# State-space block and SiLU layer on one core: decay factors of the first two units spread over the partitions by products with 0/1 matrices, and a new instruction list

## The chip, the core and the metric

The kernel runs on one core of one Trainium2 chip. A core has a matrix engine (TensorE, PE in the profile; its weight loads are PEld), a vector engine (VectorE, DVE), an activation engine (ScalarE, ACT), a general engine (GpSimd, POOL), and a queue engine (SyncE, SP) that here only issues DMA transfers. They run side by side and wait for one another by semaphores. On-chip data lies in a memory of 128 partitions; TensorE writes its results to a separate accumulator memory (PSUM). The metric is the device time of one execution in microseconds (us), smaller is better. A product of float32 operands shows in the trace as two matmul records on PE; one of operands marked float32r shows as one.

## What is computed

The reference is a chunked state-space scan per batch and head, whose output goes through a two-layer network with a SiLU between.

```python
batch, H, S, D, N = 4, 8, 768, 32, 16      # x: (4,8,768,32)  a: (4,8,768)  B, C: (4,8,768,16)
log_a = log(clip(a, 1e-6, 1)); state = 0
for each chunk of the sequence:
    cum = cumsum(log_a[chunk])
    L   = exp(cum_i - cum_j), causal                  # product of a between j and i
    y   = ((C B^T) * L) @ x  +  (C @ state) * exp(cum)
    state = exp(sum log_a) * state + sum_j exp(cum_last - cum_j) * B_j x_j
x2  = y as (3072, 256)
h   = x2 @ w_in                                       # w_in: (256, 2048)
out = (h * sigmoid(h)) @ w_out                        # w_out: (2048, 256)
```

The two weight matrices arrive as 64-bit floats and have to be rebuilt as 32-bit ones on the chip. The output is (3072, 256) in float32.

## The kernel before, in words

The work is cut into 12 units of 256 sequence positions (3 per batch). For a unit, the state-space part is: load B and C in two layouts (`Ln`, `Lt`), x (`Lx`) and the factors a in two layouts; run prefix products of a along the sequence, once as a table of 128 x 512 per half unit (`E`, f_E, line 481, a scan on DVE against a `diag` pattern) and once per chunk (`P01`/`P`, lines 446 and 453); multiply B by the last column of the table (`B`, line 489, on POOL); transpose C and B (`T` line 494 on DVE, `tp` line 500 on PE); form the small products of B, C and x (`g0` line 556, `D`/`gd` line 542), multiply with the table (`M`, line 571), carry the state (`S`, lines 584 and 586, and `SM`, line 594), and add up the unit's output (`Y`, lines 607 and 616), which ScalarE copies out (`X0` line 646, `y` line 652).

The network then takes the outputs two units at a time. The first pair (units 0 and 1) goes through it in plain float32: `s,u,j` (f_s1, line 676) is the first layer for unit u and the 256 hidden columns of weight block j, `si` (line 682) the SiLU, `n` (line 744) the second layer. The other five pairs go through products of operands split into three float32r parts: `a` and `d` (line 785) with `ax` (796) and `dg` (806) for the first layer; `h` (812), `l` (633), `e` (636) split its result; `f` (766) is the second layer.

Each of the 16 weight blocks (`lw,n`: 0 to 7 of w_in, 8 to 15 of w_out, 512 KB each, in 7 buffers) is rebuilt by two ScalarE steps (`u` line 283, `v` line 286), three DVE steps (`w,n,0` line 292, `w,n,1` line 296, `w,n,2` line 299) and an addition on GpSimd (`W`, line 310, some in two halves), then split for the later pairs (`H` line 314, `Wd` line 322 on ScalarE, `Wl` line 319 on GpSimd, `We` line 326 an accumulating DMA that GpSimd issues).

**Where the factors a come from.** Units 2 to 11 read them from two scratch tensors in DRAM, `az` and `ac`: all of a is loaded by four DMAs (`ir`, line 350), clamped on GpSimd (`AA`, line 429), and written out (`AD`, lines 435 and 437). Units 0 and 1 cannot wait for that. For the per-chunk products, `ip,u,q` (line 346) loads 8 heads' factors with each row repeated onto 16 partitions, 128 KB, straight into 128 partitions; DVE clamps it (`P01,u,0`, line 442) and scans it (`P01,u,1`, line 446). For the table, `ia` (line 342) loads a as 32 rows of 2 x 64; DVE clamps it (`A`, line 415), PE transposes it (`AT`, line 420), DVE copies the result (`AU`, line 424); `as,u,k` (f_AS) then spreads each column to 128 x 512, once on DVE (line 464) and three times on ScalarE (line 466), and `ab,u,k` (f_Ab, line 471) transposes that by four PE transposes, so that every partition holds the wanted row.

**What sets the order.** There is no scheduler: the string SCHEDULE lists some 1,400 tokens, each a call of one of these functions, and each engine runs its own instructions in the list's order. A token `z` is dummy matmuls that keep PE running (lines 408 and 410). The third or last number of `Ln`, `Lt`, `Lx`, `ip`, `lw` names the queue that issues the DMA: 0 SyncE, 1 ScalarE, 2 GpSimd. SLOTS lists, for each kind of buffer, which of its places each new tile takes. The list's first tokens are

```text
c1 ip,0,0 Ln,0,0,0,1 ci ia lw,0 z,1 cp cI z,1 ch z,1 z,0,6 Lt,0,1,2,1 z,0,6 z,0,6 z,1 Lt,0,1,0,1 Lt,0,1,3,1 z,1
Lt,0,1,1,1 cd lw,2 co z,1 Ln,0,0,1,1 z,1 Ln,1,0,0,0 P01,0,0 ct A ip,1,0 z,1 P01,0,1 Lx,0,0,0 Lx,0,1,0 AT u,0 AU
Ln,1,0,1,0 ca z,1 as,0,0 z,1 as,1,1 z,1 ab,0,0 Ln,1,1,0,0 z,0,6 cP as,0,1 w,0,0 T,0,1 Ln,1,1,1,0 C,0 as,1,0 Lx,1,0,0
```

The small constants are built at the start: `ci` (idle, line 355), `c1`/`cd` (diag, 366 to 372), `cI` (identity, 361), `ch` and `cP` (head mask and par, 381 to 389), `cp` and `co` (patterns for the scans, 376 to 393), `ct` (line 358, a one-column SiLU that makes ScalarE load its function table).

Of the kernel before, what the change touches and what calls it, by code (L numbers as in the profile page):

```python
# [13 lines left out]
ALU = mybir.AluOpType  # L14
# [16 lines left out]
ce,2,1 tq,2 W,9,1,0 n,2 w,11,2 si,0,3 u,6 Lt,3,0,3,0 ce,2,0 E,2,1 Wl,4 lw,7 W,10,1,0 n,1 E,2,0 lw,12 AD,1 n,1 v,7 n,1
w,5,1 P,2 C,2 g0,2 B,2 W,5,1,0 gd,2 b,2,0 La,3,0,0 M,2,1 b,2,1 Lt,3,0,1,0 Lx,3,0,0 La,3,1,0 AD,2 u,7 u,12 Ln,3,0,1,0
W,11,1,0 S,2,0 w,6,0 Lt,3,0,2,0 w,7,2 Lt,3,0,0,0 Lt,4,1,0,0 M,2,0 Ln,3,0,0,0 n,1 Lt,4,1,1,0 Lp,3,0 ce,3,0 S,2,1 S,2,2
H,11 lw,14 w,7,0 w,7,1 n,2 s,0,5 ce,3,1 w,6,2 SM,2,1 E,3,0 SM,2,0 Y,2 Lx,3,1,0 si,0,5 n,1 v,12 n,1 W,7,1,0 n,1 H,1 H,9
E,3,1 lw,13 y,2,0 n,1 y,2,1 s,0,7 B,3 xh,2 x,2,0 T,3,0 H,5 g0,3 Wd,0 w,6,1 P,3 H,10 Lt,4,0,3,0 w,12,2 gd,3 La,4,0,0
si,0,7 b,3,0 M,3,1 w,12,0 Wd,9 Lt,4,0,1,0 Lt,4,0,2,0 b,3,1 La,4,1,0 S,3,0 S,3,1 W,6,1,0 Lt,4,1,2,0 s,0,6 Wl,11 si,0,6
v,13 C,3 M,3,0 S,3,2 w,12,1 Wl,5 Lt,4,1,3,0 SM,3,0 SM,3,1 x,2,1 u,13 H,8 Lp,4,0 n,1 We,0 s,1,6 W,12,1,0 Y,3 T,4,1
lw,15 w,13,2 n,2 Wl,3 y,3,0 Ln,4,0,0,0 Lt,4,0,0,0 y,3,1 xh,3 n,1 w,13,0 Lx,5,1,0 x,3,0 x,3,1 S,3,3 a,1,0 E,4,1
Ln,4,0,1,0 si,1,6 s,1,5 w,13,1 We,2 v,15 Lx,4,0,0 P,4 AD,3 n,1 u,15 ce,4,1 W,13,1,0 T,4,0 w,15,0 ax,1,0 u,14 E,4,0
d,1,0 ce,4,0 si,1,5 H,6 v,14 w,14,0 H,7 dg,1,0 Lx,4,1,0 Wl,10 H,12 w,14,1 C,4 w,15,1 Lp,5,0 s,1,7 w,14,2 B,4 si,1,7  # L40
g0,4 W,14,1,0 h,1,0 gd,4 M,4,1 n,1 Lx,5,0,0 b,4,0 b,4,1 S,4,0 n,1 Wd,1 S,4,1 S,4,2 Wd,12 Lt,5,0,2,0 Wl,1 We,1 n,2
M,4,0 Lt,5,1,3,0 Wd,5 SM,4,0 La,5,1,0 n,1 SM,4,1 Y,4 Wl,8 w,15,2 e,1,0 n,1 Wd,3 Wl,7 y,4,1 H,13 f,1 a,1,1 y,4,0 We,4
# [843 lines left out]
```

## Time and profile before

| quantity | value |
|---|---|
| median of 3 runs | 331.68 us (331.28 to 333.41) |
| the profiled execution's own time | 331.95 us |
| its span on the core, from first to last recorded event | 330.2 us |
| mean granted TensorE clock | 0.998 |
| instructions recorded | 7573 |
| PE, PEld busy | 319.5, 243.8 us |
| DVE, ACT, POOL busy | 240.8, 207.4, 88.8 us |
| DMA | 95,817 packets, 30.83 MB, 80,088 packets under 512 bytes |

The page gives each engine's busy time and its course in 40 slices of 8.25 us. The chain of waits names the work that ended last at each moment; the timeline lists instructions in order of time; the windows give busy time by stretch. A busy PE need not be a PE at its peak, since the ends of matmul records are modelled.

### The profile page before, as it was taken

Reading aid. Unit: us, or ns where it says so; the run is one execution under the profiler, and the core shown is the slowest. Engines: PE = TensorE matmul, PEld = TensorE weight load, DVE = VectorE, ACT = ScalarE, POOL = GpSimd, SP = SyncE. Lnnn points to the kernel's source line nnn. Section 1 sums busy time; section 2 is a strip of 40 time slices with the busy share of each in tenths; the row PEclk is TensorE's granted clock in tenths of the full one; section 3 lists DMA queues with packets and bytes.
Section 4 is the critical chain, followed back from the end, with each engine's and each line's share of the span. In section 5 each row is a group of like instructions: output and inputs, shape, how many; then the busy total and the mean of one; then the engine's idle time right before and its main releaser. Section 6 shows DMA issues by size and latency. Waiting matters only on the chain.

```text
span 330.2 us, 7573 instructions
## 1 busy us (share of the span) xinstructions
PE 319.5 (97%) x3086; PEld 243.8 (74%) x3086; DVE 240.8 (73%) x314; ACT 207.4 (63%) x323; POOL 88.8 (27%) x96
## 2 busy tenths in 40 slices
PE   7699999999999999999999999999999999999995
PEld 3478746665667778877878878778887788888883
DVE  4979899999957972978589469688648534555563
ACT  3689928578787558565756566655664737474441
POOL 2367853978969510020010100200000000000000
PEclk9999999999999999999999999999999999999999
DMA  6799699594696991412422441450003100005002
GB/s 170 121 339 222 184 219 206 142 193 102 129 185 98 196 173 35 99 47 45 99 25 64 74 97 24 92 102 11 2 0 65 18 0 2 0 0 89 0 0 64
DMA packets 95817, 30.83 MB, mean 93 GB/s; under 512 B 80088, under 2 KB 87000, under 8 KB 95784
## 3 DMA queue, kind: packets, MB, share of 16 engines
q1 hardware_dynamic: 90632, 25.58, 36.1%
q0 software_dynamic: 2480, 4.39, 7.4%
q10 hardware_dynamic: 2672, 0.39, 0.7%
q8 instruction: 24, 0.39, 0.5%
q14 instruction: 9, 0.07, 0.1%
HBM read 22.81 MB, written 3.34 MB: 79 GB/s over the span
## 4 chain that ended last, share of the span: by engine, by line
PE 88%; DVE 4%; DMA 3%; SPq 2%; ACT 1%; issue 1%; POOL 1%; DVEq 0%
PE hp L766 28%; PE ga L785 17%; PE gb L785 17%; PE hp L676 7%; PE o_ps L766 6%; PE hp L744 5%; PE ga L616 2%; PE ga L556 2%; PE ga L607 1%; DMA raw<-in_moe_w_in_dram 1%; DVE s2k L292 1%; DMA s2k<-in_C_dram 1%; PE ga L542 1%; PE gb L607 1%; SPq L258 1%
## 5 line engine op out<-in xcount | busy, mean ns | idle before, releaser
L766 PE MATMUL hp<-r4k,s2k 128*128 128x512 f32 x400 | 113.3, 394 | 0.0
L766 PEld LDWEIGHTS hp<-r4k,s2k 128*128 128x128 f32 x400 | 74.4, 188 | 16.5 <-issue 0.6
L633 DVE SCALAR_TENSOR_TENSOR r4k<-r4k,r4k 128x1024 fp32r<-128x1024 f32 x40 | 50.9, 1278 | 30.1 <-PE hp L766 16.8
L636 DVE SCALAR_TENSOR_TENSOR r4k<-r4k,r4k 128x1024 fp32r<-128x1024 f32 x40 | 49.7, 1247 | 27.2 <-ACT r4k L812 15.2
L785 PE MATMUL ga<-raw,s2k 128*128 128x512 f32 x240 | 62.8, 397 | 0.0
L785 PE MATMUL gb<-raw,s2k 128*128 128x512 f32 x240 | 61.8, 393 | 0.0
L785 PEld LDWEIGHTS ga<-raw,s2k 128*128 128x128 f32 x240 | 44.6, 188 | 12.2 <-issue 1.2
L785 PEld LDWEIGHTS gb<-raw,s2k 128*128 128x128 f32 x240 | 44.4, 188 | 11.2 <-ACT gb L796 1.0
L812 ACT ACTIVATE r4k<-r4k 128x1024 fp32r<-128x1024 f32 x40 | 41.8, 1055 | 4.3 <-PE hp L766 2.6
L796 ACT ACTIVATE ga<-ga 128x1024 f32<-128x1024 f32 x20 | 20.2, 1009 | 32.6 <-PE ga L785 32.6
L796 ACT ACTIVATE gb<-gb 128x1024 f32<-128x1024 f32 x20 | 20.2, 1008 | 17.9 <-PE gb L785 16.9
L766 PE MATMUL o_ps<-r4k,s2k 128*128 128x512 f32 x80 | 31.2, 396 | 0.0
L744 PE MATMUL hp<-r4k,s2k 128*128 128x512 f32 x64 | 29.8, 600 | 0.7 <-POOL s2k L310 0.7
L676 PE MATMUL hp<-r4k,s2k 128*128 128x256 f32 x128 | 29.5, 382 | 0.0
L489 POOL TENSOR_TENSOR BT<-bn,ab 128x256 f32<-128x256 f32 x10 | 9.4, 939 | 72.0 <-PE hp L766 27.8
L676 PEld LDWEIGHTS hp<-r4k,s2k 128*128 128x128 f32 x128 | 23.9, 190 | 5.0 <-issue 1.0
L310 POOL TENSOR_TENSOR s2k<-s2k,s2k 128x512 uint32<-128x512 uint32 (+1 forms) x19 | 24.1, 1277 | 11.3 <-DVE s2k L299 5.8
L520 POOL TENSOR_TENSOR cw<-ct,pfx 128x256 f32<-128x256 f32 x9 | 9.5, 1053 | 64.8 <-DVE pfx L453 64.8
L806 ACT ACTIVATE r4k<-ga 128x1024 f32<-128x1024 f32 x20 | 20.5, 1024 | 9.8 <-PE ga L785 4.3
L481 DVE TENSOR_TENSOR_SCAN ab<-ab,diag 128x512 f32<-128x512 f32 x20 | 26.0, 1316 | 0.8 <-DMA ab<-az 0.8
L806 ACT ACTIVATE r4k<-gb 128x1024 f32<-128x1024 f32 x20 | 20.4, 1022 | 6.8 <-PE gb L785 5.7
L319 POOL TENSOR_TENSOR s2k<-s2k,s2k 128x512 fp32r<-128x512 f32 x16 | 24.0, 1568 | 0.8 <-ACT s2k L314 0.8
(118 smaller groups left out, 399.0 us busy)
## 6 DMA issues: line engine op xcount, KB each, us to landing
ab<-az SPq DMA_DIRECT2D x20, 256.0 KB
raw<-in_moe_w_in_dram SPq DMA_DIRECT2D x8, 512.0 KB
raw<-in_moe_w_out_dram SPq DMA_DIRECT2D x8, 512.0 KB
s2k<-s2k POOLq DMA_DIRECT2D x16, 256.0 KB, 5.4
out_dram<-r4k SPq DMA_DIRECT2D x44, 64.0 KB
xt<-in_x_dram SPq DMA_DIRECT2D x20, 128.0 KB
pz<-ac SPq DMA_DIRECT2D x10, 130.0 KB
bn<-in_B_dram SPq DMA_DIRECT2D x20, 64.0 KB
```

Source lines behind the costliest of these rows:

```text
L310: nc.gpsimd.tensor_tensor(out=dst[:, :, fs].bitcast(U32), in0=u[:, :, fs], in1=v[:, :, fs], op=ALU.add)
L319: nc.gpsimd.tensor_tensor(out=t, in0=f32(WK[n, "h"]), in1=WT[n], op=ALU.add)
L481: nc.vector.tensor_tensor_scan(out=o, data0=src, data1=diag.rearrange("p h t -> p (h t)"), initial=0.0, op0=ALU.mult, op1=ALU.add)
L633: nc.vector.scalar_tensor_tensor(out=l, in0=f32(h), scalar=BACK, in1=y, op0=ALU.mult, op1=ALU.add)
L636: nc.vector.scalar_tensor_tensor(out=d, in0=f32(h), scalar=-(BACK + 1.0), in1=y, op0=ALU.mult, op1=ALU.subtract)
L676: nc.tensor.matmul(out=hp[:, i], lhsT=WT[j][:, kc, 128 * i:128 * i + 128], rhs=XM[:, 2 * kc:2 * kc + 2, u], start=(kc == 0), stop=(kc == K ...
L744: nc.tensor.matmul(out=NP["o"][m], lhsT=WT[8 + f // 2][:, f % 2, 128 * m:128 * m + 128], rhs=GT[0, f // 2][:, f % 2], start=(f == 0), stop ...
L766: nc.tensor.matmul(out=ACC[P, 2 * (p == "d") + m], lhsT=WK[8 + f // 2, p][:, f % 2, 128 * m:128 * m + 128], rhs=rhs, start=(f == 0 and p ! ...
L785: nc.tensor.matmul(out=o, lhsT=WK[j, q][:, kc, 128 * i:128 * i + 128], rhs=xs[:, 2 * kc:2 * kc + 2], start=(start and q == "h" and kc == 0 ...
L796: nc.scalar.activation(t, t, AF.Copy, scale=1.0 + Z)
L806: nc.scalar.activation(g, t, AF.Silu, scale=BACK)
L812: nc.scalar.activation(t, GT[G, i], AF.Copy, scale=-LESS * Z)
```

## The change

Units 0 and 1 get their factors in another way, and the whole list (SCHEDULE and SLOTS) is a new one.

- `ip` is now one DMA: 8 heads x 512 positions, 16 KB, on 8 partitions. GpSimd clamps each unit's half (`PA`), one product on PE with the 0/1 matrix `spread` (8 x 128) puts each head's row on 16 partitions (`pb`), and DVE scans it from PSUM (`P01`). The two 128 KB loads and DVE's two clamps are gone.
- `ia` loads the 32 chunk rows of all 8 heads, 64 KB, into partitions 96 to 127 of a 128 x 512 tile `ar`; `zr` sets the other 96 partitions to zero; DVE clamps the tile (`A`). `ab,u,k` is one product on PE of the full height of 128 with 128 columns of the 0/1 matrix `pick`, instead of a spread copy and four transposes. `AT`, `AU` and the four `as` copies are gone.
- GpSimd builds `pick` (128 x 512, token `cs`) and `spread` (8 x 128, `c2`) by a memset and two selects each.
- In the new list one of the four `ir` loads is the third DMA that SyncE issues; `lw,2` comes ahead of `lw,0`; `ct` comes after `ab,1,0`, so that the first ScalarE function is a `ce` copy; and the order of the rest differs throughout. The number of `z`, `s`, `n`, `a`, `d`, `f` steps' matmuls is the same.

```diff
-    ach = small([32, 2, Q])
-    aT = small([128, 8, 4])
+    ar, pr = small([128, H, Q]), small([H, 2 * UT])
+    pick, spread = small([128, 4 * 128]), small([H, 128])
...
     def i_a():
-        nc.sync.dma_start(out=ach, in_=bass.AP(tensor=a.tensor, offset=a.offset,
-                                               ap=[[Q, 8], [2 * S, 4], [S, 2], [1, Q]]))
-    def i_p(u, q):
-        QUEUES[q].dma_start(out=pa[u], in_=bass.AP(tensor=a.tensor, offset=a.offset + UT * u,
-                                                   ap=[[S, H], [0, N], [1, UT]]))
+        nc.sync.dma_start(out=ar[96:128], in_=bass.AP(tensor=a.tensor, offset=a.offset,
+                                                      ap=[[Q, 32], [S, H], [1, Q]]))
+    def c_rest():
+        nc.vector.memset(ar[0:96], 0.0)
+    def i_p(q):
+        QUEUES[q].dma_start(out=pr, in_=bass.AP(tensor=a.tensor, offset=a.offset, ap=[[S, H], [1, 2 * UT]]))
...
+    def band(t, n, w, p0=0):
+        nc.gpsimd.memset(t, 1.0)
+        nc.gpsimd.affine_select(out=t, in_=t, pattern=[[1, n]], compare_op=ALU.is_ge,
+                                fill=0.0, base=w * p0, channel_multiplier=-w)
+        nc.gpsimd.affine_select(out=t, in_=t, pattern=[[-1, n]], compare_op=ALU.is_ge,
+                                fill=0.0, base=w - 1 - w * p0, channel_multiplier=w)
...
     def f_A():
-        nc.vector.tensor_scalar(out=ach, in0=ach, scalar1=1.0, scalar2=1e-6, op0=ALU.min, op1=ALU.max)
-        nc.vector.memset(ach[:, :, 0:1], 0.0)
-    def f_AT():
...
-    def f_AU():
...
+        nc.vector.tensor_scalar(out=ar, in0=ar, scalar1=1.0, scalar2=1e-6, op0=ALU.min, op1=ALU.max)
+        nc.vector.memset(ar[:, :, 0:1], 0.0)
...
-    def f_P01(u, what):
-        if what == 0:
-            nc.vector.tensor_scalar(out=pz01[u][:, :, 1:], in0=pa[u].rearrange("p (c t) -> p c t", c=4),
-                                    scalar1=1.0, scalar2=1e-6, op0=ALU.min, op1=ALU.max)
-            return
+    def f_PA(u):
+        nc.gpsimd.tensor_scalar(out=pz01[u][:, :, 1:], in0=pr[:, UT * u:UT * u + UT].rearrange("p (c t) -> p c t", c=4),
+                                scalar1=1.0, scalar2=1e-6, op0=ALU.min, op1=ALU.max)
+    def f_pb(u):
+        AB["p", u] = t = take("hp", [128, 4, Q + 1])
+        nc.tensor.matmul(out=t.rearrange("p c t -> p (c t)"), lhsT=spread, rhs=pz01[u].rearrange("p c t -> p (c t)"),
+                         start=True, stop=True)
+    def f_P01(u):
...
-                                     data0=pz01[u].rearrange("p c t -> p (c t)"),
+                                     data0=AB["p", u].rearrange("p c t -> p (c t)"),
...
-    def f_AS(u, k):
...
     def f_Ab(u, k):
         AB[u, k] = t = take("hp", [128, H, Q])
-        for j in range(4):
-            nc.tensor.transpose(out=t[:, 2 * j:2 * j + 2].rearrange("p h t -> p (h t)"),
-                                in_=AS[u, k][:, j].rearrange("p c q -> p (c q)"), identity=ident)
+        f = 128 * (2 * u + k)
+        nc.tensor.matmul(out=t.rearrange("p h t -> p (h t)"), lhsT=pick[:, f:f + 128],
+                         rhs=ar.rearrange("p h t -> p (h t)"), start=True, stop=True)
```

The new list begins

```text
ip,0 ia cs ci ir,3 c1 ch c2 Ln,0,0,0,1 z,1 cI z,1 z,1 Lt,0,1,2,1 Lt,0,1,0,1 zr z,0,6 z,0,6 A z,0,6 z,1 cd lw,2 cP cp
Lt,0,1,1,1 z,1 z,1 PA,0 z,1 z,1 z,1 pb,0 Lt,0,1,3,1 ab,0,0 T,0,1 ab,0,1 P01,0 Ln,0,0,1,1 ab,1,1 Lx,0,0,0 lw,0 Lx,0,1,0
PA,1 ce,0,0 v,2 C,0 u,2 z,1 u,0 z,1 z,0,6 Ln,1,0,1,0 E,0,0 Ln,1,1,0,0 E,0,1 E,1,1 Ln,1,0,0,0 ce,0,1 w,0,0 B,0,0 z,0,6
B,0,1 z,0,6 Ln,1,1,1,0 tp,0 tq,0 D,0 g0,0 S,0,0 Lt,3,1,1,0 S,0,1 v,0 pb,1 w,2,0 S,0,2 Lx,1,0,0 M,0,1 M,0,0 Lx,1,1,0
ir,0 ab,1,0 ct co lw,1 w,2,1 w,2,2 SM,0,1 SM,0,0 B,1,1 tp,1 ce,1,1 tq,1 Y,0 ce,1,0 X0,0,0 S,0,3 X0,0,1 E,1,0 P01,1
lw,3 W,2,2,0 W,2,2,1 H,2 u,1 w,0,2 B,1,0 w,0,1 g0,1 v,1 lw,4 D,1 S,1,0 S,1,1 S,1,2 v,3 SM,1,0 M,1,0 s,0,2 M,1,1 w,1,0
SM,1,1 W,0,2,0 ir,1 w,1,2 lw,10 u,3 Lt,3,1,3,0 W,0,2,1 ir,2 w,1,1 s,0,0 si,0,0 C,1 u,4 S,1,3 w,3,0 W,1,2,0 lw,9 lw,8
v,4 w,3,2 W,1,2,1 w,3,1 Y,1 lw,11 X0,1,1 X0,1,0 u,10 s,0,1 w,4,0 Ln,2,1,1,0 H,0 s,1,2 Wl,2 w,4,2 AA,0 Ln,2,0,1,0
si,0,2 si,0,1 s,1,0 u,9 v,10 w,4,1 AD,4 w,9,0 Ln,2,0,0,0 W,3,1,0 w,10,0 v,9 W,4,1,0 si,1,2 H,3 s,1,1 si,1,1 u,8 s,1,4
```

More of the change, by code (lines that the diff above doesn't have):

```diff
@@ L94 @@
-os,5,1,0,0 or,5,1,1 os,5,1,1,1
+ip,0 ia cs ci ir,3 c1 ch c2 Ln,0,0,0,1 z,1 cI z,1 z,1 Lt,0,1,2,1 Lt,0,1,0,1 zr z,0,6 z,0,6 A z,0,6 z,1 cd lw,2 cP cp
+Lt,0,1,1,1 z,1 z,1 PA,0 z,1 z,1 z,1 pb,0 Lt,0,1,3,1 ab,0,0 T,0,1 ab,0,1 P01,0 Ln,0,0,1,1 ab,1,1 Lx,0,0,0 lw,0 Lx,0,1,0
+PA,1 ce,0,0 v,2 C,0 u,2 z,1 u,0 z,1 z,0,6 Ln,1,0,1,0 E,0,0 Ln,1,1,0,0 E,0,1 E,1,1 Ln,1,0,0,0 ce,0,1 w,0,0 B,0,0 z,0,6
+B,0,1 z,0,6 Ln,1,1,1,0 tp,0 tq,0 D,0 g0,0 S,0,0 Lt,3,1,1,0 S,0,1 v,0 pb,1 w,2,0 S,0,2 Lx,1,0,0 M,0,1 M,0,0 Lx,1,1,0
@@ L330 @@
     QUEUES = (nc.sync, nc.scalar, nc.gpsimd)
-    ach = small([32, 2, Q])
-    aT = small([128, 8, 4])
+    ar, pr = small([128, H, Q]), small([H, 2 * UT])
+    pick, spread = small([128, 4 * 128]), small([H, 128])
     araw, azt = small([NCH, H, Q]), small([NCH, H, Q])
     acp = large([NCH, H, Q + 1])
-    pa = [small([128, UT]) for _ in range(2)]
-    pz01, pfx01 = ([small([128, 4, Q + 1]) for _ in range(2)] for _ in range(2))
+    pz01 = [small([H, 4, Q + 1]) for _ in range(2)]
+    pfx01 = [small([128, 4, Q + 1]) for _ in range(2)]
     one01 = small([128, 4, Q + 1])
```

177 lines of the change are left out of this document (82 added, 95 removed), and 6 rows, old and new, of the table SLOTS.

## The prediction, made before the changed kernel was run

> **What bounds the kernel now.** I read the page first, for the engines' shares and their course over the 40 slices, then the chain of waits in order of time.
>
> ```profile
> PE 319.5 (97%) x3086; PEld 243.8 (74%) x3086; DVE 240.8 (73%) x314; ACT 207.4 (63%) x323; POOL 88.8 (27%) x96
> POOL 2367853978969510020010100200000000000000
> ```
>
> ```profile
> 2.47 4.75 DMA raw<-in_moe_w_in_dram
> 7.24 2.79 SPq L258
> 10.07 0.97 SPq L243
> 11.08 4.26 DMA s2k<-in_C_dram
> 19.01 3.65 PE hp L676 x16
> 24.07 10.56 PE hp L676 x48
> ...
> 72.61 0.86 PE hp L744 x2
> ...
> 320.10 4.53 PE hp L766 x20
> ```
>
> The columns of the chain are start, length, and what the end hung on. Up to 15.3 us it is loads: a weight block, then x, B and C on SyncE's queue. From 19.0, where the first `s` begins, it is PE almost without a break to 324.6. So the time is a front of 19 us in which little of PE's work gets done, some 305 us of PE's own work, and a tail of 5.6 us. The change leaves PE's real work as it is; it can gain by starting the `s` steps earlier and by removing gaps after that. The windows say how large the gaps are (columns: stretch, its length, busy us and instructions of each engine, clock, DMA share, GB/s).
>
> ```profile
> 10.00:15.00 5.00, 2.75 (x72) 1.70 (x72) 5.00 (x11) 2.28 (x7) 1.44 (x3) 1.00 0.81 104
> 15.00:20.00 5.00, 4.14 (x159) 3.30 (x160) 4.16 (x10) 2.95 (x9) 3.66 (x5) 1.00 0.87 252
> 45.00:50.00 5.00, 4.77 (x67) 2.61 (x67) 4.87 (x8) 2.63 (x7) 4.10 (x4) 1.00 1.09 209
> 50.00:60.00 10.00, 9.58 (x184) 6.11 (x183) 9.93 (x15) 7.46 (x18) 4.65 (x4) 1.00 0.80 189
> 60.00:70.00 10.00, 9.28 (x116) 6.11 (x116) 9.89 (x15) 6.78 (x15) 8.90 (x8) 1.00 0.84 171
> ```
>
> Between 45 and 70 us PE is idle 0.23 + 0.42 + 0.72 = 1.37 us, while DVE is busy nearly all the time. The clock is granted in full. That, and whatever stalls hide under the modelled ends of the matmuls, is what a better sequence has to win behind the front.
>
> **The front, part by part.** The timeline, with start, length and what ended the idle time before:
>
> ```profile
> 1.93 0.35 POOL L362 TENSOR_SCALAR_AFFINE_SELECT ident<-ident 128x128 f32<-128x128 f32 x1 [0.29 <-DVE ident L361]
> 4.04 1.28 ACT L358 ACT_TABLE_LOAD   x1 [4.04 <-DMA s2k<-in_B_dram]
> 4.19 0.29 DVE L442 TENSOR_SCALAR s2k<-s2k 128x256 f32<-128x256 f32 x1 [2.06 <-DMA s2k<-in_a_dram]
> 4.94 0.21 DVE L415 TENSOR_SCALAR s2k<-s2k 32x128 f32<-32x128 f32 x1 [0.46 <-DMA s2k<-in_a_dram]
> 5.20 0.69 DVE L446 TENSOR_TENSOR_SCAN s2k<-s2k,s2k 128x260 f32<-128x260 f32 x1
> 6.01 0.43 DVE L464 COPY s2k<-s2k 128x512 f32<-128x512 f32 x1
> 6.67 0.60 PE L471 MATMUL hp<-ident,s2k 128*128 128x128 f32 x4
> 7.82 1.65 ACT L466 ACTIVATE s2k<-s2k 128x512 f32<-128x512 f32 x3
> 7.95 0.43 DVE L292 TENSOR_SCALAR s2k<-s2k 128x512 f32<-128x512 f32 x1 [1.38 <-ACT s2k L283]
> 8.29 0.64 DVE L494 STREAM_TRANSPOSE ct<-s2k 128x256 f32<-128x256 f32 x1
> 9.11 3.43 DVE L481 TENSOR_TENSOR_SCAN ab<-hp,diag 128x512 f32<-128x512 f32 x3
> 15.39 0.51 PE L500 MATMUL o_ps<-ident,s2k 128*128 128x128 f32 x2 [1.69 <-DMA s2k<-in_C_dram]
> 15.61 1.22 DVE L481 TENSOR_TENSOR_SCAN ab<-hp,diag 128x512 f32<-128x512 f32 x1
> ```
>
> *PE.* The trace has no 512-column plain float32 product in the front; the `n` steps have (72.61 us, two records, 0.86 us). So each `ab` costs 0.86 us against 0.60 for four transposes: four cost 1.0 us more. The two `pb`, 260 columns, cost by width 0.44 each, and `AT` goes. All this replaces PE time that holds dummies or stands idle (2.25 us from 10 to 15 and 0.86 from 15 to 20 in the windows). I cost it at nothing; without that cover it would be 1.9 us.
>
> *GpSimd* gains `pick`: a memset and two selects of 128x512. The 128x128 select took 0.35; four times that, 1.4, is a ceiling for each, 0.35 the floor; with a fixed part in it I take 0.7, so 2.1 in all. With `spread` (three steps of at most 0.35) that is 3.1 us at the start of GpSimd's queue, where `c1` and `ch` stood, and `PA,0` runs at 5 to 6 us, with `pb` behind it. That is in time for the first scans, next.
>
> *DVE* loses two clamps (2 x 0.29), the small clamp, `AU` and the 0.43 copy, and gains the clamp of 128x512 (0.43, as L292 has it) and a memset of 96x512 while it waits for the load. Its order is now: `A` after the load at about 4.9, `cd` and small constants (0.8), `T` (0.64), `P01` (0.69), then the three `E` scans. That lets them start at 7.5 to 8.5 against 9.11. But L292 and L296 of one weight block, done before them until now, come behind them: some 0.7 given back. `E,1,0`, at 15.61 before, comes at 15.2 or so. *ScalarE* loses three copies (1.65) and gains a table load, below.
>
> *Loads.* Ahead of the last C block on SyncE's queue stood
>
> ```profile
> s2k<-in_a_dram SPq DMA_DIRECT2D x2, 128.0 KB
> s2k<-in_a_dram SPq DMA_DIRECT2D x4, 24.0 KB
> s2k<-in_a_dram SPq DMA_DIRECT2D x1, 16.0 KB
> ```
>
> 2 x 128 + 16 = 272 KB of a; now 16 + 64 + 24 (the `ir` moved up) = 104. At the 252 and 104 GB/s of the windows the missing 168 KB are 0.7 or 1.6 us, and nothing if queue issue (SPq in the chain), not bytes, sets it: that C block is the eleventh DMA in both orders. I take 0.7. The transposes at 15.39, which waited 1.69 us for C and stand ahead of `Y,0` on PE, then run at 14.7; DVE's 15.2 for `E,1,0` allows about the same. **The first `s` comes 0.7 us earlier, at 18.3; bounds 0 and 1.6.**
>
> **Behind the front.** PE wants the weights 0.7 us earlier too. One place looks tight. `s,1,4` is now the seventh `s` step, ahead of `s,0,4`, and needs `W4`. On GpSimd's queue `W4` now stands behind `Wl,2`, `AA,0`, the DMA issue of `az`, and `W3`; before, it stood ahead of `az`.
>
> ```profile
> 26.58 1.07 POOL L429 TENSOR_SCALAR s2k<-s2k 48x512 f32<-48x512 f32 x1 [2.07 <-DMA s2k<-in_a_dram]
> 27.71 0.27 POOL L431 MEMSET s2k<- 48x8 f32 x1
> 29.09 1.33 POOL L310 TENSOR_TENSOR s2k<-s2k,s2k 128x512 uint32<-128x512 uint32 x1
> 30.36 0.77 POOL L435 DMA_DIRECT2D az<-s2k  x1
> ```
>
> `AA,0` waited for a until 26.58. With the `ir` loads as late, `W4` ends at 26.58 + 1.07 + 0.27 + 0.77 + 2 x 1.33 = 31.3. PE reaches `s,1,4` after six steps of eight records, 1.76 each (10.56/6), and `Y,1` (24.07 - 19.01 - 3.65 = 1.4): 18.3 + 10.6 + 1.4 = 30.3, a wait of 1.0. But an `ir` load is now third on the queue and the last stands behind one weight block fewer, so `AA,0` should start at about 25 to 26, and the wait is 0 to 1.0; I take **+0.4**.
>
> Later the list has less DVE work ahead of the same PE steps, because `E,2`, `az` and the weights 8 to 10 come earlier. I give it half of the 1.37 us: **-0.6**, bounds 0 and -1.4. The tail keeps its steps in their order (the last stores go in the same way): 0.
>
> Sum: -0.7 + 0.4 - 0.6 = -0.9. The profiled execution took 331.95 us, of which 330.2 are its span, and 0.27 more than the median of 331.68. So 331.05 for such an execution, **330.8 us** as a median.
>
> **Rivals.** *GpSimd out of DVE's way (faster).* DVE's steps are slow where a GpSimd addition runs:
>
> ```profile
> 29.21 1.49 DVE L292 TENSOR_SCALAR s2k<-s2k 128x512 f32<-128x512 f32 x1
> ...
> L292 DVE TENSOR_SCALAR s2k<-s2k x16: 404/848/1932, 8.0 to 75.1; 128x512 f32<-128x512 f32 x16
> ```
>
> 0.40 us is the quickest of 16, 0.85 the median; the one at 29.21 starts inside the addition at 29.09 and ends 0.28 after it. If the new sequence keeps the two apart, DVE gets up to 16 x (0.85 - 0.40) = 7 us back from this line alone, nearly all of it before 80 us. DVE's rows of the windows are full there, so all 1.37 us of idle PE go, the front gains its full 1.6 instead of 0.7, W4's wait goes, and some hidden stalls with it: 331.7 - 1.6 - 1.4 = 328.7, and 327.7 with one us of hidden ones, my guess. Against it: GpSimd has as many additions as before, and `W8`, `W9`, `W10` now stand side by side on its queue. The Trainium skill, SBUF — State Buffer, section "Who interferes with whom", says that the second to issue "fully blocks" until the first is done; by that rule, which the row agrees with (0.40 to 1.49), the selects of `pick` can also hold DVE's clamp at the start, up to 0.7 us by my estimate of one.
>
> *ScalarE's queue in the front (slower).* `u,0` stands ahead of `ce,0,1` and `tq,0` and waits for a weight block that is now second in line; and a second table load (1.28 in the row, with 0.2 for `ct`) stands ahead of `SM`, which stands ahead of `Y,0`. If `lw,0` lands after about 10.5 us, `tq` ends after 11.8, `v,0` and the load end past 14, and `Y,0` begins at 16.7 instead of the 15.2 that the loads allow (14.7 + 0.5 for the transposes): the first `s` at 19.8 instead of 18.3, thus 330.8 + 1.5 = 332.3, and 333 with W4's wait in full. The Trainium skill, ScalarE: Activation LUTs, section "What ACT_TABLE_LOAD costs", counts 1.38 us of drain on top of such a load; by that page the case would be 334.4. The trace shows no drain there.
>
> *The new list stalls PE in the middle (slower).* GpSimd runs its steps in order, and `Wl,15`, `Wl,13`, `We,13` to `We,15` now stand behind `B,6` and `C,6`, which wait for DVE. If those come a run of three (3 x 1.3, by L310) later than PE can bear, PE loses 4.0 us: 330.8 + 4.0 = 334.8, and 335.2 if W4's wait is nearly its full 1.0. It decides only if GpSimd is late there; before, it is busy at most two tenths of any slice from the fifteenth (115 us) on.
>
> *It doesn't do what it says:* the front is bound by the queue's issue, GpSimd and DVE collide as before: 331.7.
>
> **How the numbers follow.** About 1%, 3.3 us, is what a measurement tells from no change. My forecast has 0.33, the last rival 0.12, and both lie within 1%. GpSimd out of the way has 0.22, and 0.18 of it beyond 1%, since stalls hidden in a busy PE may be larger than I guess. ScalarE's queue has 0.15, a third of it beyond 1%; the stall in the middle 0.18, of which 0.17 beyond. That is 0.18 faster, 0.6 same, 0.22 slower. The range goes from the faster rival's 327.7 to the stall's 335.2, each with about half its outer cases left out, 0.2 together.
>
> **What would show it.** Right: the first scan L481 below 8.5, the transposes behind C at about 14.7, the first L676 at 18.3, and a chain on PE from there. Wrong: `SM` behind a table load with PE idle, a wait of L676 on L310 near 30 us, or PE idle beyond 100 us behind GpSimd. L292's median tells of the first rival.

## The result, and the profile after

The changed kernel takes 329.65 us (median of 15 executions, 329.32 to 330.90) against 331.68 us for the kernel before, timed beside it (15 executions): a ratio of 0.9937, 95% interval 0.9919 to 0.9954. The profiled execution took 329.56 us, 327.5 of them its span, 2.64 us less than the span before. The ratios in the experiments' table leave out slow executions, more than 1.5% above the fastest of their kernel: one of e4 and two of e9.

First the page of the changed kernel, its engines and GpSimd's course over the 40 slices:

```profile
PE 321.0 (98%) x3081; PEld 244.3 (75%) x3081; DVE 238.4 (73%) x311; ACT 207.7 (63%) x321; POOL 90.2 (28%) x104
POOL 6467847658967343210100101010010000000000
```

GpSimd is busier than before (90.2 us against 88.8), above all in the first slice (6 tenths against 2), where `pick` is made. VectorE has 2.4 us less to do. The chain of waits shows more (start, length, what the end hung on):

```profile
1.27 1.46 PE o_ps L417 x3
...
3.83 2.33 PE o_ps L417 x6
6.17 0.63 PE hp L446 x2
6.79 2.77 PE hp L468 x6
9.57 0.43 PE o_ps L417 x2
...
12.99 1.10 PE hp L468 x2
14.09 0.44 PE o_ps L497 x4
...
17.63 3.65 PE hp L673 x16
```

Before, this chain ran over loads and their issue up to 15.3 us. Now it is nearly all TensorE from 1.27 us on: dummies (L417), the `pb` products (L446), the `ab` products (L468); at 11.09 us ScalarE has 0.40 us of it (line 506). The view of TensorE's waits between 9 and 20 us says the same, first of the kernel before:

```profile
PE o_ps L500 <- DMA s2k<-in_C_dram: 1.7, 1, 1.7
PE ga L556 <- ACT bh L509: 0.5, 1, 0.5
PE ga L556 <- ACT r4k L646: 0.5, 1, 0.5
```

and of the changed one, where the wait for C is gone:

```profile
PE ga L553 <- ACT r4k L643: 0.5, 1, 0.5
```

Why C comes earlier is seen in SyncE's own rows, of the kernel before:

```profile
5.12 1.08 SPq L346 DMA_DIRECT2D s2k<-in_a_dram  x1
...
11.08 1.27 SPq L243 DMA_DIRECT2D s2k<-in_C_dram  x2
```

and of the changed one:

```profile
0.82 0.39 SPq L349 DMA_DIRECT2D s2k<-in_a_dram  x1
...
9.84 0.58 SPq L243 DMA_DIRECT2D s2k<-in_C_dram  x1
```

SyncE took 0.80 and 1.08 us to issue the two loads that repeat rows, and takes 0.39 us for the one load in their place. The last C load of units 0 and 1 on this queue is the eleventh DMA in both kernels; it was issued by 12.35 us before and by 10.42 us now, 1.9 us earlier.

The timeline has the steps that the prediction named: `T`, the first three `E` scans, and the transposes behind C.

```profile
7.00 0.64 DVE L491 STREAM_TRANSPOSE ct<-s2k 128x256 f32<-128x256 f32 x1 [1.89 <-DMA s2k<-in_x_dram]
...
8.04 3.42 DVE L478 TENSOR_TENSOR_SCAN ab<-hp,diag 128x512 f32<-128x512 f32 x3
...
13.92 0.60 PE L497 MATMUL o_ps<-ident,s2k 128*128 128x128 f32 x4
```

The windows, in the columns used before:

```profile
10.00:15.00 5.00, 4.80 (x148) 3.18 (x152) 4.88 (x12) 3.80 (x10) 1.19 (x4) 1.00 0.86 119
45.00:50.00 5.00, 5.00 (x17) 2.94 (x16) 4.65 (x9) 5.00 (x12) 1.22 (x1) 1.00 0.96 210
50.00:60.00 10.00, 10.00 (x186) 6.58 (x185) 9.97 (x11) 5.70 (x14) 8.01 (x8) 1.00 0.65 160
60.00:70.00 10.00, 9.28 (x120) 6.84 (x119) 7.86 (x14) 7.82 (x17) 5.31 (x5) 1.00 0.77 186
```

TensorE is busy 4.80 us of the stretch from 10 to 15 (2.75 before). From 45 to 60 us its idle 0.65 us are gone. From 60 to 70 it idles 0.72 us in both kernels, for different reasons, below.

By how much the changed kernel is ahead, counted from TensorE's records at equal work done: 1.38 us at the first `s` step (17.56 against 18.94); 1.07 from `s,1,4` at 30 us until 43; 1.9 at 54; 2.0 to 2.1 from 60 to 90; 2.5 at 125; 2.64 at the end. This is an account of two executions. The medians differ by 2.03 us, and another execution of the old front (e8 below, whose list is the same up to `lw,1`) reaches its first `s` at 18.54 us, 0.98 behind the changed kernel and not 1.38.

### The profile page after: what moved, and what is told of

Its sections match the earlier page's. It is cut to its first block, busy times and chain, and to the rows that moved or that the text cites. A ratio compares the mean times of both kernels' runs of the same rounds, so it can differ in the third digit from the quotient of the medians.

```text
span 327.5 us, 7562 instructions
## 1 busy us (share of the span) xinstructions
PE 321.0 (98%) x3081; PEld 244.3 (75%) x3081; DVE 238.4 (73%) x311; ACT 207.7 (63%) x321; POOL 90.2 (28%) x104
## 4 chain that ended last, share of the span: by engine, by line
PE 88%; DMA 4%; DVE 4%; issue 1%; ACT 1%; SPq 1%; POOL 0%; DVEq 0%
PE hp L763 29%; PE ga L782 17%; PE gb L782 17%; PE o_ps L763 6%; PE hp L673 4%; PE hp L741 4%; DMA ac<-r4k 2%; PE ga L613 2%; PE ga L553 2%; DMA ab<-az 2%; PE ga L604 1%; PE o_ps L417 1%; PE hp L468 1%; PE gb L604 1%; PE ga L539 1%
## 5 line engine op out<-in xcount | busy, mean ns | idle before, releaser
L763 PEld LDWEIGHTS hp<-r4k,s2k 128*128 128x128 f32 x400 | 74.3, 188 | 16.2 <-issue 0.6
L630 DVE SCALAR_TENSOR_TENSOR r4k<-r4k,r4k 128x1024 fp32r<-128x1024 f32 x40 | 49.1, 1230 | 31.5 <-ACT r4k L809 23.9
L633 DVE SCALAR_TENSOR_TENSOR r4k<-r4k,r4k 128x1024 fp32r<-128x1024 f32 x40 | 50.1, 1257 | 16.5 <-ACT r4k L809 10.3
L478 DVE TENSOR_TENSOR_SCAN ab<-ab,diag 128x512 f32<-128x512 f32 x20 | 28.3, 1425 | 3.3 <-DMA ab<-az 3.3
L673 PEld LDWEIGHTS hp<-r4k,s2k 128*128 128x128 f32 x128 | 23.8, 190 | 5.5 <-issue 1.9
L741 PEld LDWEIGHTS hp<-r4k,s2k 128*128 128x128 f32 x64 | 11.8, 189 | 9.6 <-issue 7.9
```

What stands on the lines that cost most here:

```text
L478: nc.vector.tensor_tensor_scan(out=o, data0=src, data1=diag.rearrange("p h t -> p (h t)"), initial=0.0, op0=ALU.mult, op1=ALU.add)
L630: nc.vector.scalar_tensor_tensor(out=l, in0=f32(h), scalar=BACK, in1=y, op0=ALU.mult, op1=ALU.add)
L633: nc.vector.scalar_tensor_tensor(out=d, in0=f32(h), scalar=-(BACK + 1.0), in1=y, op0=ALU.mult, op1=ALU.subtract)
L673: nc.tensor.matmul(out=hp[:, i], lhsT=WT[j][:, kc, 128 * i:128 * i + 128], rhs=XM[:, 2 * kc:2 * kc + 2, u], start=(kc == 0), stop=(kc == K ...
L741: nc.tensor.matmul(out=NP["o"][m], lhsT=WT[8 + f // 2][:, f % 2, 128 * m:128 * m + 128], rhs=GT[0, f // 2][:, f % 2], start=(f == 0), stop ...
L763: nc.tensor.matmul(out=ACC[P, 2 * (p == "d") + m], lhsT=WK[8 + f // 2, p][:, f % 2, 128 * m:128 * m + 128], rhs=rhs, start=(f == 0 and p ! ...
```

## The experiments

My theory after the result: some 1.4 us from the front, because the factors a come with less loading and no copies; some 0.3 lost at `W4`; the rest from the order behind the front, above all the earlier az. The rivals: all of it from the order; all of it from the new way to bring a; all of it from fewer bytes on the queue.

The twelve runs, each timed beside the kernel before ("first `s`" and "end" tell how many us later than in the changed kernel's profile the first `s` step and the end come in the run's profile; "clock" is the mean granted TensorE clock over the executions):

| run | median, range (us) | ratio to before, 95% | clock | first `s` | end |
|---|---|---|---|---|---|
| e1 new way, old order | 337.83 (336.45–339.05) | 1.0165 (1.0126–1.0205) | 0.982–0.990 | +7.78 | +9.14 |
| e2 old way, new order | 337.55 (336.21–338.47) | 1.0154 (1.0116–1.0191) | 0.978–0.988 | +7.44 | +8.50 |
| e3 more bytes | 331.77 (330.77–333.40) | 0.9996 (0.9973–1.0018) | 0.995–1.000 | +2.23 | +2.75 |
| e4 fewer dummies | 331.92 (329.90–335.25) | 0.9981 (0.9952–1.0009) | 0.990–1.000 | −0.43 | +3.52 |
| e5 new way, old order, again | 334.78 (332.39–336.35) | 1.0071 (1.0042–1.0099) | 0.983–1.000 | +4.38 | +4.78 |
| e6 old way, new order, again | 331.32 (330.39–334.02) | 0.9998 (0.9968–1.0027) | 0.982–0.999 | +2.44 | +3.23 |
| e7 late az | 330.44 (329.48–332.89) | 0.9953 (0.9928–0.9979) | 0.997–1.000 | +0.30 | +0.65 |
| e8 early az, old kernel | 332.29 (331.17–333.83) | 1.0006 (0.9983–1.0029) | 0.987–0.999 | +0.98 | +2.58 |
| e9 products of 32 rows | 330.52 (329.71–335.76) | 0.9949 (0.9927–0.9971) | 0.973–1.000 | +0.22 | +0.23 |
| e10 `pb` of 128 rows | 329.76 (329.52–330.05) | 0.9926 (0.9898–0.9953) | 0.997–1.000 | +0.31 | +0.49 |
| e11 two waits | 329.70 (328.86–330.11) | 0.9922 (0.9896–0.9948) | 0.998–1.000 | −0.12 | +0.23 |
| e12 changed, again | 329.64 (329.50–330.33) | 0.9928 (0.9903–0.9953) | 0.997–1.000 | −0.27 | +0.11 |

**The new way without the new order (e1, e5).** The new functions, in the old list:

```diff
-c1 ip,0,0 Ln,0,0,0,1 ci ia lw,0 ... ch ... cd ... P01,0,0 ct A ip,1,0 z,1 P01,0,1 ... AT u,0 AU ... as,0,0 ...
+ip,0 Ln,0,0,0,1 ci ia cs c1 lw,0 ... ch c2 ... zr cd ... PA,0 ct A z,1 PA,1 pb,0 P01,0 ... u,0 ...
-P01,1,0 ... P01,1,1
+pb,1 ... P01,1          (e1: pb,1 in buffer 2 of hp; e5: in buffer 0)
```

> The new way to bring a (products with pick and spread) in the old order of steps. If the gain has two parts, the front (1.38 us at the first s step, because a arrives with less loading and without the copies) and the order behind it (about 1.2 us more by 125 us), this kernel gets some of the first and none of the second: first s step near 18.0 to 18.5 instead of 18.94, time 330.7 to 331.2 us. If the new order alone is the cause: first s step at 18.9, time 331.7 or more. If the new way alone is: 329.7 us.

> The new way to bring a in the old order again, with pb,1 in the buffer that is free first: in the first try it had to wait 3.24 us for VectorE to leave its buffer, and the granted clock fell to 0.5 for 6 us. Two parts (front and order behind it): no TensorE gap over 2 us, granted clock 1.00 throughout, time 330.5 to 331.5 us. New order alone: 331.7 us or more. New way alone: 329.7 us. If the old order's dummies and loads do not fit the new way at all: a first s step after 20 us, 333 us or more.

In e1 `pb,1` waited 3.24 us for a buffer, and the windows (columns as above, granted clock third from the end) show what followed:

```profile
16.00:18.00 2.00, 0.30 (x1) 0.00 (x0) 2.00 (x7) 0.48 (x2) 0.00 (x0) 1.00 0.98 288
18.00:20.00 2.00, 0.46 (x2) 0.29 (x2) 1.40 (x3) 0.16 (x1) 1.77 (x3) 1.00 1.04 382
20.00:22.00 2.00, 2.00 (x71) 1.38 (x70) 1.28 (x2) 0.95 (x3) 0.39 (x1) 0.63 1.01 354
22.00:24.00 2.00, 1.54 (x46) 1.35 (x50) 0.00 (x0) 1.23 (x4) 1.01 (x2) 0.50 1.04 276
```

After the idle stretch the clock is 0.50, for some 6 us: one wait was paid twice. In e5 `pb,1` still waits, but 1.3 us, and the profile keeps its clock; e5 too is slower than the kernel before, by 0.7%. Its chain shows where its front is lost:

```profile
3.83 2.25 PE o_ps L415 x5
6.08 1.16 PE hp L444 x2
7.24 1.39 PE o_ps L415 x3
8.63 1.71 PE hp L466 x2
10.34 0.49 PE o_ps L417 x12
10.83 1.91 PE hp L466 x4
```

The dummies that filled TensorE's wait for the old copies now stand in front of the products, and the first product took 0.85 us per record (1.71 / 2) where the next two took 0.48 (1.91 / 4), at a granted clock shown as 1.00. The first `s` comes at 21.94 us: of the four cases expected for e5, the one that came is that the old order's dummies and loads do not fit the new way. In the old order, then, the new way is a loss, and the rival "all from the way" falls; what the way is worth by itself, with dummies placed for it, e5 does not tell.

**The new order with the old way (e2, e6).** The old functions in the new list; e2 had three load issues behind copies on ScalarE's queue, e6 has them ahead:

```diff
-ip,0 ia cs ci ... c1 ch c2 ... zr ... PA,0 z,1 z,1 z,1 pb,0 ... P01,0 ... lw,0 Lx,0,1,0 PA,1 ... pb,1 ... P01,1
+ip,0,0 ia ci ... c1 ch ... AT AU as,0,0 as,0,1 as,1,1 z,1 z,1 z,1 P01,0,0 ... P01,0,1 ... lw,0 ip,1,0 Lx,0,1,0 as,1,0 ... P01,1,0 ... P01,1,1
```

> The old way to bring a (two loads of repeated rows, a transpose and copies) in the new order of steps. Two parts: the front is as late as before or later, first s step 18.5 to 19.0, the order behind it still closes gaps between 45 and 70 us, time 330.4 to 330.9 us. New order alone: first s step near 17.6, 329.7 us. New way alone: 331.7 us.

> The old way to bring a in the new order again, with ScalarE's three load issues ahead of its copies: in the first try they stood behind the copies, and a block of C came 5 us late. Behind 40 us this kernel should keep its distance to the changed one (as the first try did: 8.43 us at 40 us, 8.50 at the end), so that its time is 329.65 plus what it loses in the front. Two parts: front 1 to 2 us later than with the new way, 330.6 to 331.6 us. New order alone: 329.7 us. New way alone: 331.7 us, and gaps between 45 and 55 us as before the change.

Both kernels lie behind the changed one in the front, by more than expected, and from 40 us on the distance stands nearly still: e2 8.44 us at 40 us, 8.50 at the end; e6 3.05 and 3.23. Part of the front's loss is the clock: in the profile of e6, one of its slower executions (332.82 us), the granted clock is 0.50 from 12 to 20 us, in that of e2 from 16 to 26. e1 goes from 8.44 to 9.14 and e5 from 4.07 to 4.78, with the old order. So the order behind the front is worth 0.7 us even to a kernel that reaches it late. e6 as a whole takes 330.75 us in the seven executions with a clock of 0.995 or more, and 332.8 to 334.0 in the five at 0.982 or 0.983. Even the better ones are 1.1 us above the changed kernel, though some 0.7 us below the kernel before where that keeps its clock (331.41 us, table below): the order alone does not give the changed kernel's time either.

**Bytes (e3).** Two loads of 128 KB of a's rows are put back, into tiles that are not read then:

```diff
-ip,0 ia cs ci ... lw,0 Lx,0,1,0
+im,0 ip,0 ia cs ci ... lw,0 im,1 Lx,0,1,0
```

> The changed kernel with the two loads of 128 KB put back on SyncE's queue, into tiles that nobody reads yet: only their bytes and their issue. If the 0.7 us of the prediction's front came from 168 KB less in the queue, the transposes behind C and the first s step come some 0.7 us later (18.2 to 18.3 instead of 17.56), time about 330.4 us. If TensorE's own products and dummies set the front of the changed kernel, as its chain of waits has it: first s step within 0.2 us of 17.56, time 329.6 to 329.9 us.

Neither expectation held: the first `s` came 2.23 us late. Its chain:

```profile
3.83 2.67 PE o_ps L422 x6
6.50 1.16 PE hp L451 x2
7.66 4.31 PE hp L473 x6
```

The same six records of products took 4.31 us against 2.77, and dummies and products together 1.88 us more. In TensorE's records a dummy of 512 columns takes 0.427 us at first and 0.213 later; the change falls at 5.6 us in the changed kernel and at 10.7 in e3. So most of the 2.23 in this profile is TensorE's rate, and what the loads cost the time is not isolated. What they cost the queue is: over all fourteen profiles SyncE had issued the last of the C loads by 11.20 to 12.35 us where the two loads of repeated rows stand (before, e2, e3, e6, e8), and by 10.13 to 11.08 us in the nine without them, in the old order (e1, e5) as in the new.

**Dummies (e4).** The two wide and eighteen narrow dummies after `ab,1,1` are left out:

```diff
-u,2 z,1 u,0 z,1 z,0,6 ... B,0,0 z,0,6 B,0,1 z,0,6
+u,2 u,0 ... B,0,0 B,0,1
```

> The changed kernel without the two wide and eighteen narrow dummy products between ab,1,1 and the first transposes, 1.12 us in its trace. If TensorE's own order sets the front: first s step up to 1.1 us earlier (16.5 to 17.0), time 328.6 to 329.1 us. If the scans on VectorE or GpSimd's steps behind them set it: first s step within 0.2 us of 17.56, time 329.5 to 329.8 us. If the dummies keep the clock up: granted clock below 1.0 in the first 20 us and a later front, 330 us or more.

The first `s` gained 0.43 us of the 1.12: VectorE's three scans (3.45 us from 7.58) then end the chain. Later the gain was lost, in the chain and the windows:

```profile
22.46 1.60 issue
```

```profile
22.00:24.00 2.00, 0.34 (x7) 0.20 (x7) 1.35 (x2) 2.00 (x5) 1.92 (x3) 1.00 1.02 362
24.00:26.00 2.00, 1.94 (x29) 1.60 (x30) 2.00 (x4) 1.50 (x5) 1.61 (x4) 0.70 1.06 397
26.00:28.00 2.00, 2.00 (x6) 1.56 (x5) 1.83 (x2) 0.93 (x2) 1.02 (x2) 0.50 0.94 169
```

In the middle of `Y,1` TensorE stood 1.60 us without a wait that the profile shows, and the clock fell to 0.50. A 16 KB read of instructions began at 21.72 us there (18.43 in the changed kernel). Whether it caused the stall was not tried; a shorter stall in e11 (below) began 2 us after such a read (19.87 us), and e10 has a read at 19.80 us and no stall. Seven of e4's twelve executions have a clock of 0.995 or less, where the changed kernel has none below 0.997; the five others have a median of 330.42 us, also above the changed kernel's. So these dummies do not cost what their 1.12 us suggest.

**az (e7, e8).**

```diff
 e7, changed kernel:
-w,4,1 AD,4 w,9,0 Ln,2,0,0,0 W,3,1,0 w,10,0 v,9 W,4,1,0
+w,4,1 w,9,0 Ln,2,0,0,0 W,3,1,0 w,10,0 v,9 W,4,1,0 AD,4
 e8, kernel before:
-lw,1 S,0,2 ... ir,3 ... ir,2 ... ir,1 ir,0 ... AA,0 v,4 ... AD,4
+lw,1 ir,3 ir,2 ir,1 ir,0 S,0,2 ... AA,0 AD,4 v,4
```

> The changed kernel with one step moved: the issue of az on GpSimd's queue behind W3 and W4 instead of ahead of them, as before the change, some 3.5 us later. If az, and with it the scans E,2, is what closed the gaps between 45 and 55 us: the wait of s,1,4 for W4 (0.31) goes, and 0.5 to 0.9 us of TensorE time come back as idle before 60 us; 329.8 to 330.3 us. If az had slack: only the wait for W4 goes, 329.3 to 329.5 us.

> The kernel before with the four loads for az right behind lw,1 on SyncE's queue and the issue of az right behind its clamp on GpSimd's queue. If an early az is what the new order gains behind the front: the gaps at 45 to 55 us (0.65 us idle in the windows) close, 330.6 to 331.2 us. If not, or if the weight blocks that these loads delay matter more: 331.7 to 332.7 us.

TensorE's waits behind 30 us, before the change:

```profile
PE hp L744 <- POOL s2k L310: 0.7, 1, 0.7
...
PE ga L616 <- ACT sm L594: 0.4, 1, 0.4
PE ga L542 <- POOL BT L489: 0.2, 1, 0.2
```

In e8 exactly the last of these is gone (0.23 us), the two others stay, and it loses 1.27 us behind 38 us against 1.57 of the kernel before; its median does not show it, and its 332.29 us lie in the range expected if an early az is not the gain. In the changed kernel one wait is left, and in e7 it is longer:

```profile
PE ga L613 <- ACT sm L591: 0.7, 1, 0.7
```

```profile
PE ga L612 <- ACT sm L590: 1.0, 1, 1.0
```

e7's front was 0.31 us late, but `s,0,4` began with the changed kernel's, since the wait for `W4` had gone. So in these profiles az's place is worth 0.2 to 0.3 us in the old list (e8) and 0.3 to 0.5 us in the new one (e7: the longer wait; the distance at 70 us), not the whole gain, and in e7 at 63 us, not at the place that I named (45 to 55 us).

e8's profile shows another thing. The wait for C is there (1.7 us, from 12.8 on), and behind it the granted clock (third from the end) falls:

```profile
12.00:14.00 2.00, 0.83 (x7) 0.60 (x6) 2.00 (x7) 0.00 (x0) 0.41 (x1) 1.00 0.77 102
14.00:16.00 2.00, 1.52 (x89) 1.27 (x89) 2.00 (x4) 1.73 (x5) 1.13 (x2) 1.00 0.64 138
16.00:18.00 2.00, 1.53 (x48) 1.09 (x47) 1.66 (x4) 0.69 (x3) 1.37 (x3) 0.62 0.92 279
18.00:20.00 2.00, 2.00 (x36) 1.60 (x37) 1.21 (x4) 1.57 (x3) 1.46 (x3) 0.53 0.95 312
```

The profiled execution of the kernel before has the same wait and keeps its clock. Over all 74 of its executions beside e1 to e12:

| granted clock | kernel before | changed kernel |
|---|---|---|
| 0.996 or more | 32 executions, median 331.41 us | 21 of 21, median 329.65 us |
| 0.991 to 0.995 | 18, median 332.21 | none |
| 0.990 or less | 24, median 332.99 | none |

Over all, the medians are 332.0 and 329.65. Some 1.75 us of the 2.35 are there at full clock; the other 0.6 come from the executions in which the kernel before has a lower clock. (In the 15 executions of the result the difference was 2.03.) That the wait for C is what lowers the clock in them is not shown: the two are seen together in one profile alone, that of e8, an edit of this kernel. Nor does the clock tell all: three executions of e7 took 332.2 to 332.9 us at 0.997 or more, and none of them was profiled.

**Height of the products (e9, e10).**

```diff
 e9:
-lhsT=pick[:, f:f + 128], rhs=ar...
+lhsT=pick[96:128, f:f + 128], rhs=ar[96:128]..., tile_position=(96, 0)
 e10: spread and pz01 with 128 partitions, pz01 set to 0 beforehand
```

> The changed kernel with the four a products over the 32 rows that carry a (rows 96 to 127) instead of all 128. The traces so far show TensorE starting at half rate (0.427 us for a dummy of 512 columns) and changing to full rate (0.213) at 4.4 us (before; the fourth experiment), 5.6 (the changed kernel), 6.3 (late az) or 10.2 to 10.7 (first with more bytes, and new way in the old order again); in the last two the 8-row product stood in the stretch before. If products of few rows do not count as work for that gate: full rate at 10 us or later in most executions, products at 0.85 us per record, first s step 1 to 2 us later, time 330.5 to 332 us. If height does not matter: as the changed kernel, 329.4 to 329.9 us.

> The changed kernel with the two pb products over all 128 rows (rows 8 to 127 zero) instead of 8. If few rows do not count for the gate: full rate by 7.7 us in every execution, so the slow ones go; median 329.4 to 329.6 us and none above 330.3. If rows do not matter: same median and same spread as the changed kernel, 329.3 to 330.9 us.

The profile of e9 does not show what I expected: TensorE was at full rate from 7.0 us, and a record over 32 rows took no other time than one over 128 (one every 0.43 us in both):

```profile
7.30 2.30 PE L467 MATMUL hp<-s2k,s2k 32*128 32x512 f32 x5
```

But eight of its twelve executions have a clock of 0.993 or less, down to 0.973, where the changed kernel's 21 have none below 0.997. One reading is that rows count as work for whatever sets the clock, with an effect after the start rather than at it. It is not shown: no lowered execution of e9 was profiled, and e4, whose `ab` products have all 128 rows, has lowered clocks too. e10 gained nothing that its six executions can tell from the changed kernel's.

**Two waits (e11), and the changed kernel again (e12).** e11 is e10 with

```diff
-S,3,1 v,12 ... x,2,1 ... M,3,0 x,2,0 La,4,0,0 w,13,0 S,3,2
+S,3,1 S,3,2 v,12 ... x,2,1 ... M,3,0 x,2,0 La,4,0,0 w,13,0
-s,1,2 Wl,2 w,4,2 AA,0 ... W,3,1,0 ... W,4,1,0
+s,1,2 w,4,2 AA,0 ... W,3,1,0 ... W,4,1,0 Wl,2
```

> As the kernel before it in this list, and two steps moved: S,3,2 ahead of four other VectorE steps (Y,3 waited 0.72 us for it), and Wl,2 behind W3 and W4 on GpSimd (s,1,4 waited 0.31 us for W4). If these waits end last there, both go and TensorE keeps the 1.0 us to the end: 328.4 to 328.8 us. If the next step is as late (the a step at 66 us waits for VectorE): 329.1 to 329.5 us.

> The changed kernel once more, beside the others: median 329.5 to 329.9 us and no execution above 331 us if its executions stay as even as the first fifteen (329.32 to 330.9). If the moment of full rate falls by chance: some executions near 331.5 to 332 us, with TensorE at half rate past 10 us.

Both waits are absent in e11's profile; that for `W4` is absent in e10's as well, whose TensorE comes 0.47 us later to that step. At `s,1,5` e11 stood 0.80 us ahead of e10, at 90 us 0.2, at the end 0.26, without a wait in the view that would name the giving back. Neither expected range held. It has a new stall without a named cause at 22 us:

```profile
PE gb L603 <- issue: 0.4, 1, 0.4
```

Its median is that of e10 and e12: no version here beats the changed kernel. The six executions of e12 are as even as the first fifteen of the same kernel, which is the first of its two expectations.

## Why the prediction was right, point by point

The time lies 1.15 us below the forecast, inside its range, and within 1%.

*The front, −0.7 (0 to −1.6): 1.38.* Right in direction, too small. The scans start at 8.04, as said, and `E,1,0` at 15.08. The transposes behind C run at 13.92, not 14.7. I moved the arrival of C by what fewer bytes save, and set the queue's issue at nothing because C is the eleventh DMA in both orders; but issues differ in length (0.80 and 1.08 us against 0.39), and C was issued 1.9 us earlier. So the wait is gone as a whole, and what comes last is TensorE's own order. I costed the `ab` and `pb` products at nothing, under the cover of TensorE's idle time; the idle time closed up, and they lie on the chain. They may still cost little: 1.12 us of dummies taken out of the same stretch (e4) gave 0.43 at the first `s`.

*`W4`, +0.4 (0 to 1.0): 0.31.* Right in size, and half by luck. `W4` ends at 29.78, `s,1,4` starts at 29.84:

```profile
26.11 2.22 DVE L296 TENSOR_SCALAR s2k<-s2k 128x512 uint32<-128x512 uint32 x1
...
28.40 1.38 POOL L310 TENSOR_TENSOR s2k<-s2k,s2k 128x512 uint32<-128x512 uint32 x1 [0.37 <-DVE s2k L296]
...
29.84 2.24 PEld L673 LDWEIGHTS hp<-r4k,s2k 128*128 128x128 f32 x11 [0.44 <-POOL s2k L310]
```

`AA,0` no longer waits for its load (24.63 us), and GpSimd, done with `W3` at 28.02, then stood 0.37 us idle ahead of `W4`, for VectorE's step of 2.22 us, which overlaps `W3` and takes 0.43 in the median. Without that, `W4` would have ended at about 29.4, just when TensorE's weight load was ready for it (29.84 less the 0.44 us in its row). The queue that I named counts as well: with az moved behind `W4` (e7) the wait is gone.

*Behind the front, −0.6 (0 to −1.4): 1.57 from 43 us to the end.* TensorE's named waits account for 0.6 of it: those of 0.4 and 0.2 us (0.38 and 0.23 in the timeline) are gone, and the one of 0.72 was replaced by another of 0.72. The other 1.0 is spread over records up to 262 us and was not traced to a cause. The remaining wait shows how GpSimd still holds VectorE:

```profile
55.75 3.42 DVE L458 TENSOR_TENSOR_SCAN pfx<-pz,one 128x260 f32<-128x260 f32 x1
```

```profile
56.09 2.51 POOL L319 TENSOR_TENSOR s2k<-s2k,s2k 128x512 fp32r<-128x512 f32 x2
```

A scan that takes 0.69 us in the median of ten takes 3.42 beside two GpSimd additions; `S,3,2`, `SM,3` and `Y,3` follow late.

*The step that failed: "The clock is granted in full."* I read it from one execution. In 42 of the 74 executions of the kernel before the granted clock is 0.995 or less, in none of the changed kernel's 21. So a term was missing, some 0.6 us of the pooled medians' difference of 2.35. The Trainium skill, TensorE: Matmul & The Clock Gate, section "HAM oscillation — how this bites in real kernels", warns of idle gaps over some 3.4 us. Here a gap of 1.7 us (e8), with TensorE partly idle before it, was followed by a lower clock.

*The rivals.* GpSimd out of VectorE's way: L292's median did fall to half (848 to 420 ns), as that rival asked, its mean from 873 to 659:

```profile
L292 DVE TENSOR_SCALAR s2k<-s2k x16: 395/420/1530, 11.4 to 81.3; 128x512 f32<-128x512 f32 x16
```

But the mean of L296 rose from 657 to 739 ns and that of the 20 scans from 1316 to 1425: slow steps moved from one line to others. ScalarE's queue: the second table load does stand ahead of `SM` (12.07 to 13.35 us), but the only wait of TensorE that the view lists from 9 to 20 us is the 0.5 us shown, not one for `SM`. A stall in the middle: beyond 70 us TensorE waits once, 0.5 us in the tail, as before. That the change does nothing: e12 repeats its ratio.

## What to carry to other kernels

Before pricing an edit in a front, ask which of TensorE's idle gaps it closes, and look at the granted clock of several executions, not only of the profiled one: a gap of 2 us may cost a second time in some of them. On a queue of DMAs count how long each issue takes, not how many DMAs stand ahead. Products and dummies on an idle TensorE have cover only as long as something else is last; when loads get faster, price them again. A new way and an order can need each other: together they gave 2.0 to 2.4 us here, while the way in the old order made the median worse by 0.7% (e5) and the order alone left it where it was (e6; 0.7 us better where the clock held).

## What the runs showed of the hardware

TensorE starts at half rate (a dummy of 512 columns every 0.427 us, later every 0.213) while the profile shows a granted clock of 1.00. The full rate came at 4.4 us (before, e4), 5.6 (changed), 6.3 (e7), about 7 (e9, e10), and past 10 us in e1, e2, e3 and e5 (10.2 in e5, 10.7 in e3); the changed kernel and e4 have the same instructions until then, so it differs between executions. The Trainium skill, TensorE: Matmul & The Clock Gate, section "What's actually happening", says that the gate looks at free-running windows of 3.4 us. With the first dummy at 1.27 us, the spread from 4.4 to 7 us agrees; the four past 10 us ask for a whole window more, which is open. The 8-row `pb` product is not needed for it: e2 has no such product, and its dummies are still at half rate at 10.19 us.
